# A gated linear attention with an FFN: the rotated q and k of the later groups are turned by transposing DMAs and no longer by TensorE

## The chip, the cores and the metric

The kernel runs on one core of a Trainium2 chip. The metric is the device time of one execution in microseconds (us), lower is better. The times compared are of runs classed as fast (the executions of one kernel lie within 1.5% of each other). Engines: PE is TensorE (matmuls), PEld its weight load, DVE is VectorE, ACT is ScalarE, POOL is GpSimd, SP is SyncE, which in this kernel only issues DMAs.

## The reference

It is a linear attention with a complex decay per channel, of which only the real part of the state is read, followed by a gated FFN on the same tokens. Sizes: 4 batches, 8 heads, 768 steps, head size 48; so 3072 tokens of 384 columns; FFN width 1536. All in float32, with a wide tolerance that lets the kernel work in bf16.

```python
# attention, per batch and head
mag = sqrt(a_re**2 + a_im**2)
scale = minimum(mag, 0.999) / (mag + 1e-6)
a = (a_re + 1j * a_im) * scale
for t in range(S):
    state = a[t][:, None] * state + outer(k[t], v[t])
    y[t] = q[t] @ state.real
# FFN on x = y, heads side by side
g = x @ w_gate
ffn = (gelu(g) * (x @ w_val)) @ w_out
out = x + sigmoid(x @ w_res) * ffn
```

## The kernel before

The kernel cuts the tokens into 12 groups of 256 (two chunks of 128; three groups are one batch) and works in units of one or two groups: [0], [1, 2], [3, 4], [5, 6], [7, 8], [9, 10], [11]. The decay is taken into q and k: with the running sum of log-magnitudes and of phases, each q becomes a pair (cosine and sine part) of 96 columns a head, "rotated" q and k. Within a chunk the attention is then a plain masked product: scores = K Q^T, masked, times v.

Two kinds of stretch alternate. In a **gate/value stretch** (`phase_y(u)`) PE does the gate and value matmuls of unit u, and woven between them are the products and the attention of unit u + 1. In the stretch between two of them (`phase_x`) ACT works out logarithms, exponentials, arctangents and sines for the next unit, small DMAs move decays across partitions, and PE does the output matmuls.

The scores need Q and K with the 96 rotated columns on the partitions, but DVE makes them with tokens on the partitions. So both are turned. Before, TensorE does it, four heads at a time: eight transposes into one PSUM tile, an ACT copy of the q half and a DVE copy of the k half back to SBUF.

```python
pQ = ctx.enter_context(tc.tile_pool(name="pQ", bufs=2))
stt = ctx.enter_context(tc.tile_pool(name="stt", bufs=2))
xp = ctx.enter_context(tc.tile_pool(name="xp", bufs=10))
ldv = ctx.enter_context(tc.tile_pool(name="ldv", bufs=6))
# ... (other pools cut)

def products(g):                        # x0 and x1 (qE = q*E, kE = k/E) cut
    def mk(nm, src):
        def x():
            t = pQ.tile([128, C * H, 2, D], BF, tag=nm, name=nm)
            sb = T[src, g].rearrange("p (x u d) -> p x u d", u=1, d=D).to_broadcast([128, C * H, 2, D])
            nc.vector.tensor_tensor(out=t, in0=T["CS", g], in1=sb, op=OP.mult)
            T[nm, g] = t
        return x
    return [x0, mk("Q", "qE"), x1, mk("K", "kE")]

# attention(g, c): four heads of one chunk
def a():
    tp = psT.tile([128, 1024], BF, tag="tp", name="tp")
    for j in range(4):
        x = c * H + hg * 4 + j
        nc.tensor.transpose(out=tp[0:DD, j * 128:j * 128 + 128], in_=Q(x), identity=ident)
    for j in range(4):
        x = c * H + hg * 4 + j
        nc.tensor.transpose(out=tp[0:DD, 512 + j * 128:640 + j * 128], in_=K(x), identity=ident)
    qk = sqp.tile([128, 1024], BF, tag="qk", name="qk")
    nc.scalar.copy(out=qk[0:DD, 0:512], in_=tp[0:DD, 0:512])
    nc.vector.tensor_copy(out=qk[0:DD, 512:1024], in_=tp[0:DD, 512:1024])
    st["qk", hg] = qk
    at = psA.tile([128, 4, 128], FP, tag="at", name="at")
    for j in range(4):
        nc.tensor.matmul(out=at[:, j], lhsT=qk[0:DD, 512 + j * 128:640 + j * 128],
                         rhs=qk[0:DD, j * 128:j * 128 + 128], start=True, stop=True)
    atm = sqp.tile([128, 4, 128], BF, tag="atm", name="atm")
    nc.vector.tensor_tensor(out=atm, in0=at, in1=mask4, op=OP.mult)

# phase_y(u): gv = gate/value matmuls of unit u, pr = products of unit u + 1;
# the pairs say over which part of the stretch the steps of a list are spread
weave((0.0, 1.0, gv), (0.0, 0.4, pr), (0.3, 0.95, att_steps(u + 1, 0)))
```

The attention steps are emitted at high priority, and a scheduler orders each engine's instructions, so the places in the weave are not the final order.

## Time and profile before

| | before |
|---|---|
| time, median of 4 runs | 323.69 us (322.99 to 324.14) |
| PE / DVE / ACT busy | 84% / 73% / 65% of a span of 322.4 us |
| TensorE transposes of Q and K (`tp`) | 384, in sets of eight |
| gate/value stretches with two turned groups | 26.0, 26.4 and 26.3 us, PE busy 99.6 to 100% |

These are lines of the profile page of the kernel before: busy time of each engine; the granted TensorE clock in 40 slices of the span (tenths, 9 is full speed); the DMA queue that SP feeds (packets, MB, share of 16 engines' time); and four groups of instructions (line, engine, operation, output<-input, shapes, count | busy us, mean ns | idle before).

```profile
PE 272.1 (84%) x2200; PEld 170.5 (53%) x2200; DVE 234.8 (73%) x431; ACT 209.8 (65%) x353; POOL 80.5 (25%) x115
...
PEclk9995676959999999999999999999999999999998
...
q1 hardware_dynamic: 103296, 23.60, 36.8%
...
L351 ACT COPY qk<-tp 96x512 bf16<-96x512 bf16 x48 | 27.9, 580 | 17.1 <-PE tp L349 7.9
...
L346 PE MATMUL tp<-ident,Q 128*96 128x128 bf16 x192 | 20.1, 231 | 6.9 <-DVE Q L321 6.2
...
L349 PE MATMUL tp<-ident,K 128*96 128x128 bf16 x192 | 22.3, 235 | 0.0
...
L352 DVE COPY qk<-tp 96x512 bf16<-96x512 bf16 x48 | 19.8, 413 | 2.3 <-ACT qk L351 1.7
```

The page says what exists, but not what limits. That is read from the windows view: two gate/value stretches of the kernel before (147 and 192 us), each with the stretch after it. The columns are the window, its length, busy time of each engine with its number of instructions, granted clock, DMA share and GB/s.

```profile
core 0: us, PE busy (x) PEld busy (x) DVE busy (x) ACT busy (x) POOL busy (x), PEclk, DMA share, GB/s
147.02:173.00 25.98, 25.87 (x265) 16.04 (x263) 22.85 (x41) 16.91 (x30) 8.60 (x9) 1.00 0.61 77
173.00:192.59 19.59, 17.00 (x85) 9.59 (x84) 14.27 (x29) 17.14 (x28) 10.64 (x15) 1.00 0.54 84
192.59:218.95 26.36, 26.36 (x271) 15.99 (x269) 23.37 (x43) 16.70 (x30) 1.88 (x3) 1.00 0.23 37
218.95:236.33 17.38, 15.42 (x80) 8.69 (x79) 12.56 (x25) 13.51 (x21) 6.89 (x10) 1.00 0.29 56
```

In a gate/value stretch PE is busy for the whole of it at full clock. What a set of transposes really costs in PE's stream is read from PE's timeline (start us, us, engine, line, operation, output<-input, count), because the 231 ns of one transpose overlap with the next:

```profile
198.77 0.39 PE L346 MATMUL tp<-ident,Q 128*96 128x128 bf16 x4
199.00 0.39 PE L349 MATMUL tp<-ident,K 128*96 128x128 bf16 x4
199.22 0.39 PE L356 MATMUL at<-qk 96*128 96x128 bf16 x4
199.44 0.38 PE L443 MATMUL vp<-xT,wv 128*128 128x512 bf16 x1
```

Starts are 0.22 us apart: four transposes take 0.22 us of the stream, so a set of eight takes 0.445 us.

### The profile page before, as it was taken

The numbers are of one execution on the slowest core, as the hardware profiler recorded it, in microseconds if no ns is written. First come the engines' busy times: TensorE is split into PE (matmuls) and PEld (weight loads), VectorE is DVE, ScalarE is ACT, GpSimd is POOL, SyncE is SP. The second block draws the span as 40 slices with busy tenths as digits, with TensorE's granted clock in tenths as the row PEclk, the third lists the DMA queues.
The fourth block names the chain that finished last, engine by engine and source line by source line (L and its number), as shares of the span: only waits on it lengthen the run. The fifth ranks groups of instructions, "written<-read, shape, count | busy, mean of one in ns | idle before, by whom it ended". The sixth has DMA issues, their size and how long they took to land.

```text
span 322.4 us, 5853 instructions
## 1 busy us (share of the span) xinstructions
PE 272.1 (84%) x2200; PEld 170.5 (53%) x2200; DVE 234.8 (73%) x431; ACT 209.8 (65%) x353; POOL 80.5 (25%) x115
## 2 busy tenths in 40 slices
PE   0337927789887999789997999998999999899994
PEld 0116624677543666445664556554656655555682
DVE  2446769968499995599982999974899837864352
ACT  4549684646998557977568976569665683656150
POOL 1206522022040370259020572000630003200220
PEclk9995676959999999999999999999999999999998
DMA  8999999989999995396850595000360003600441
GB/s 159 218 183 181 182 169 165 185 174 180 187 179 186 223 160 33 76 197 113 122 36 2 107 121 95 2 0 3 75 122 3 2 0 76 122 2 0 107 91 50
DMA packets 137755, 34.55 MB, mean 107 GB/s; under 512 B 126848, under 2 KB 137728, under 8 KB 137728
## 3 DMA queue, kind: packets, MB, share of 16 engines
q1 hardware_dynamic: 103296, 23.60, 36.8%
q0 software_dynamic: 34432, 10.59, 31.2%
q8 instruction: 17, 0.28, 0.3%
q14 instruction: 10, 0.08, 0.1%
HBM read 31.31 MB, written 9.07 MB: 125 GB/s over the span
## 4 chain that ended last, share of the span: by engine, by line
PE 56%; SPq 12%; ACT 11%; DMA 9%; DVE 6%; issue 3%; POOL 1%; ACTq 0%; DVEq 0%; POOLq 0%
PE vp L443 14%; PE gp L439 13%; SPq L136 6%; SPq L144 6%; PE op L463 6%; DMA k<-in_k_dram 4%; PE rp L455 3%; PE tp L349 3%; PE tp L346 3%; PE at L356 3%; ACT L477 3%; DMA m<-dm 3%; ACT s L124 3%; PE cst L236 2%; PE y L394 2%
## 5 line engine op out<-in xcount | busy, mean ns | idle before, releaser
L124 ACT ACTIVATE h<-gp 128x512 bf16<-128x512 f32 (+1 forms) x84 | 44.5, 536 | 38.4 <-PE gp L439 37.9
L439 PE MATMUL gp<-xT,wg 128*128 128x512 bf16 (+1 forms) x252 | 65.4, 353 | 3.4 <-ACT h L124 2.0
L443 PE MATMUL vp<-xT,wv 128*128 128x512 bf16 (+1 forms) x252 | 66.6, 353 | 0.0
L446 DVE SCALAR_TENSOR_TENSOR h<-h,vp 128x512 bf16<-128x512 bf16 (+1 forms) x84 | 49.8, 603 | 16.4 <-PE vp L443 12.0
L463 PE MATMUL op<-wo,h 128*128 128x384 bf16 x288 | 50.2, 326 | 8.1 <-ACT Ei L124 5.9
L463 PEld LDWEIGHTS <-h 128*128 128x128 bf16 x288 | 27.8, 98 | 28.7 <-issue 11.3
L351 ACT COPY qk<-tp 96x512 bf16<-96x512 bf16 x48 | 27.9, 580 | 17.1 <-PE tp L349 7.9
L359 DVE TENSOR_TENSOR atm<-at,mask 128x512 bf16<-128x512 f32 x48 | 32.9, 686 | 8.2 <-PE at L356 7.8
L472 POOL DMA_DIRECT2D out_dram<-x x22 | 20.4, 947 | 54.4 <-DMA out_dram<-ot 43.1
L439 PEld LDWEIGHTS <-wg 128*128 128x128 bf16 x252 | 23.7, 99 | 17.9 <-issue 4.2
L443 PEld LDWEIGHTS <-wv 128*128 128x128 bf16 x252 | 23.8, 99 | 13.3
L189 DVE TENSOR_TENSOR ai<-s,ai 128x768 f32<-128x768 f32 x12 | 11.1, 955 | 23.6 <-ACT s L124 23.6
L477 ACT ACT_TABLE_LOAD x21 | 26.9, 1283 | 1.1 <-PEq L615 0.7
L346 PE MATMUL tp<-ident,Q 128*96 128x128 bf16 x192 | 20.1, 231 | 6.9 <-DVE Q L321 6.2
L346 PEld LDWEIGHTS <-Q 128*96 128x96 bf16 x192 | 17.4, 130 | 15.3 <-DVE Q L321 10.0
L124 ACT ACTIVATE CS<-fg,hpi 128x768 bf16<-128x768 f32 x12 | 11.2, 935 | 20.8 <-DVE fg L246 20.7
L150 POOL DMA_DIRECT2D v<-in_v_dram x24 | 21.9, 932 | 4.2 <-DMA v<-in_v_dram 1.3
L349 PE MATMUL tp<-ident,K 128*96 128x128 bf16 x192 | 22.3, 235 | 0.0
L236 PE MATMUL cst<-ai,lt0b 128*128 128x384 f32 x24 | 11.8, 577 | 11.7 <-ACT ai L124 11.0
L352 DVE COPY qk<-tp 96x512 bf16<-96x512 bf16 x48 | 19.8, 413 | 2.3 <-ACT qk L351 1.7
L212 PE MATMUL csl<-ar,lt0a 128*128 128x384 f32 x24 | 11.4, 562 | 10.8 <-DMA ar<-in_a_re_dram 10.8
L466 DVE SCALAR_TENSOR_TENSOR ot<-sg,op 128x384 f32<-128x384 f32 x24 | 13.1, 547 | 10.1 <-PE op L463 10.1
(85 smaller groups left out, 522.0 us busy)
## 6 DMA issues: line engine op xcount, KB each, us to landing
ar<-in_a_re_dram SPq DMA_DIRECT2D x24, 192.0 KB, 4.7
ai<-in_a_im_dram SPq DMA_DIRECT2D x24, 192.0 KB, 4.1
q<-in_q_dram SPq DMA_DIRECT2D x24, 192.0 KB, 3.8
k<-in_k_dram SPq DMA_DIRECT2D x24, 192.0 KB, 3.7
out_dram<-ot SPq DMA_DIRECT2D x24, 192.0 KB, 2.5
out_dram<-x POOLq DMA_DIRECT2D x22, 192.0 KB, 3.7
v<-in_v_dram POOLq DMA_DIRECT2D x24, 96.0 KB, 5.0
wg<-in_moe_w_gate_dram POOLq DMA_DIRECT2D x4, 288.0 KB, 11.4
```

Source lines behind the costliest of these rows:

```text
L124: tab(nc.scalar.activation(**kw))
L150: nc.gpsimd.dma_start(out=t[:, c], in_=rows(v, g, c))
L346: nc.tensor.transpose(out=tp[0:DD, j * 128:j * 128 + 128], in_=Q(x), identity=ident)
L349: nc.tensor.transpose(out=tp[0:DD, 512 + j * 128:640 + j * 128], in_=K(x), identity=ident)
L351: nc.scalar.copy(out=qk[0:DD, 0:512], in_=tp[0:DD, 0:512])
L359: nc.vector.tensor_tensor(out=atm, in0=at, in1=mask4, op=OP.mult)
L439: nc.tensor.matmul(out=gp, lhsT=wg[:, fi, ffi * 128:(ffi + 1) * 128], rhs=xT[:, fi, :], start=(fi == 0), stop=(fi == KD - 1))
L443: nc.tensor.matmul(out=vp, lhsT=wv[:, fi, ffi * 128:(ffi + 1) * 128], rhs=xT[:, fi, :], start=(fi == 0), stop=(fi == KD - 1))
L446: nc.vector.scalar_tensor_tensor(out=h2[:, ffi, :], in0=h2[:, ffi, :], scalar=0.5, in1=vp, op0=OP.mult, op1=OP.mult)
L463: nc.tensor.matmul(out=ps, lhsT=h2[:, ffi, jj * 128:(jj + 1) * 128], rhs=wo[:, ffi, :], start=(ffi == 0), stop=(ffi == KF - 1))
L472: nc.gpsimd.dma_start(out=out[t0:t0 + 128, :], in_=T["x", token(u, jj)], accum_op=OP.add)
L477: tab(nc.scalar.preload_act_table_set(nm))
```

## The change

The intent is to take the turning of q and k off TensorE, ACT and DVE. DVE now writes every group's Q and K into tiles padded from 96 to 128 columns a head. From the sixth group on (g >= 5; seven of twelve groups) one transposing DMA each, issued by SP, turns a whole group's Q or K (128 x 2048 bf16, 512 KB) into `QT` or `KT`. The scores read these. The first five groups are still turned by TensorE; in their part of the span, to about 104 us, the slices show the DMA engines 80% busy and more with loads.

The padded and the turned tiles need SBUF, so the change also makes room: the mask is kept once and broadcast, the phase sums carried from group to group run in a single tile `R`, one temporary is written into its consumer's tile, `G` is a single buffer, and the pools of v and x shrink.

```diff
-    xp = ctx.enter_context(tc.tile_pool(name="xp", bufs=10))
+    xp = ctx.enter_context(tc.tile_pool(name="xp", bufs=8))
-    ldv = ctx.enter_context(tc.tile_pool(name="ldv", bufs=6))
+    ldv = ctx.enter_context(tc.tile_pool(name="ldv", bufs=5))
+    trp = ctx.enter_context(tc.tile_pool(name="trp", bufs=1))
+    pads = {}                           # two per Q and K; pad columns set to zero once
     ...
     def x():                            # products
-        t = pQ.tile([128, C * H, 2, D], BF, tag=nm, name=nm)
+        t = pads[nm, g % 2][:, :, 0:DD].rearrange("p x (u d) -> p x u d", u=2)
         nc.vector.tensor_tensor(out=t, in0=T["CS", g], in1=sb, op=OP.mult)
         T[nm, g] = t
+        if g >= TURN:                   # TURN = 5
+            tt = trp.tile([128, C * H, 128], BF, tag=nm + "T", name=nm + "T")
+            nc.sync.dma_start_transpose(out=tt, in_=pads[nm, g % 2])
+            T[nm + "T", g] = tt
     ...
+    def turned():                       # scores of four heads, in place of a()
+        x0 = c * H + hg * 4
+        st["qk", hg] = T["QT", g][0:DD, x0:x0 + 4]
+        for j in range(4):
+            nc.tensor.matmul(out=at[:, j], lhsT=T["KT", g][0:DD, x0 + j], rhs=T["QT", g][0:DD, x0 + j], ...)
+        nc.vector.tensor_tensor(out=atm, in0=at, in1=mask4, op=OP.mult)
     ...
     if s > 0:                           # carry(g): phase sum ahead of group g
-        P = stt.tile([128, DM], FP, tag="P", name="P")
-        nc.vector.tensor_tensor(out=P, in0=T["th", g - 1][:, DM:W], in1=T["th", g][:, 0:DM], op=OP.add)
-        if s > 1:
-            nc.vector.tensor_tensor(out=P, in0=P, in1=T["P", g - 1], op=OP.add)
+        P = T["R"]                      # one tile, updated again after the group's sums (carry_on)
+        nc.vector.tensor_tensor(out=P, in0=P, in1=T["th", g][:, 0:DM], op=OP.add)
     ...
-    cst = [call(carry, g) for g in g1] + [call(cs_t, g, c) for g in g1 for c in range(C)]
+    cst = [f for g in g1 for f in [call(carry, g)] + [call(cs_t, g, c) for c in range(C)]]
```

More of the change, by code (lines that the diff above doesn't have):

```diff
@@ L59 @@
     I2PI = 1.0 / (2.0 * math.pi)
+    TURN = 5
     LNMAX = 0.5 * math.log(0.998001)
@@ L82 @@
     nc.vector.memset(ones1, 1.0)
-    mask4 = singles.tile([128, 4, 128], BF, name="mask4")
-    for jm in range(4):
-        nc.vector.tensor_copy(out=mask4[:, jm, :], in_=lmat[1])
+    mask1 = singles.tile([128, 1, 128], BF, name="mask1")
+    nc.vector.tensor_copy(out=mask1[:, 0, :], in_=lmat[1])
+    mask4 = mask1.to_broadcast([128, 4, 128])
     wg = singles.tile([128, KD, FF], BF, name="wg")
@@ L90 @@
     wr = singles.tile([128, KD, DM], BF, name="wr")
+    pads = {}
+    for nm in ("Q", "K"):
+        for i in range(2):
+            pads[nm, i] = singles.tile([128, C * H, 128], BF, name="pad%s%d" % (nm, i))
+            nc.gpsimd.memset(pads[nm, i][:, :, DD:128], 0.0)
     lda = ctx.enter_context(tc.tile_pool(name="lda", bufs=6))
     ldq = ctx.enter_context(tc.tile_pool(name="ldq", bufs=4))
-    ldv = ctx.enter_context(tc.tile_pool(name="ldv", bufs=6))
+    ldv = ctx.enter_context(tc.tile_pool(name="ldv", bufs=5))
     pS = ctx.enter_context(tc.tile_pool(name="pS", bufs=2))
@@ L101 @@
     stt = ctx.enter_context(tc.tile_pool(name="stt", bufs=2))
+    st1 = ctx.enter_context(tc.tile_pool(name="st1", bufs=1))
+    trp = ctx.enter_context(tc.tile_pool(name="trp", bufs=1))
     mp = ctx.enter_context(tc.tile_pool(name="mp", bufs=3))
-    xp = ctx.enter_context(tc.tile_pool(name="xp", bufs=10))
+    xp = ctx.enter_context(tc.tile_pool(name="xp", bufs=8))
     xtp = ctx.enter_context(tc.tile_pool(name="xtp", bufs=2))
@@ L222, in carry, with carry_on @@
         if s > 0:
-            P = stt.tile([128, DM], FP, tag="P", name="P")
-            nc.vector.tensor_tensor(out=P, in0=T["th", g - 1][:, DM:W], in1=T["th", g][:, 0:DM], op=OP.add)
-            if s > 1:
-                nc.vector.tensor_tensor(out=P, in0=P, in1=T["P", g - 1], op=OP.add)
+            P = T["R"]
+            nc.vector.tensor_tensor(out=P, in0=P, in1=T["th", g][:, 0:DM], op=OP.add)
             T["P", g] = P
+    def carry_on(g):
+        s = g % NS
+        if s == 0:
+            T["R"] = st1.tile([128, DM], FP, tag="R", name="R")
+            nc.vector.tensor_copy(out=T["R"], in_=T["th", g][:, DM:W])
+        elif s < NS - 1:
+            nc.vector.tensor_tensor(out=T["R"], in0=T["R"], in1=T["th", g][:, DM:W], op=OP.add)
     def cs_t(g, c):
@@ L241, in cs_t @@
         hs = slice(c * H, (c + 1) * H)
-        r = pS.tile([128, H, D], FP, tag="r", name="r")
+        r = fg[:, hs, 0, :]
         nc.vector.tensor_scalar(out=r, in0=cs3, scalar1=MAGIC, scalar2=MAGIC, op0=OP.add, op1=OP.subtract)
@@ L245, in cs_t @@
         if c == C - 1:
+            carry_on(g)
             nc.vector.tensor_scalar(out=fg[:, :, 0, :].bitcast(mybir.dt.int32), in0=fg[:, :, 1, :].bitcast(mybir.dt.int32),
@@ L341, in grp @@
         def grp(hg):
+            def turned():
+                x0 = c * H + hg * 4
+                st["qk", hg] = T["QT", g][0:DD, x0:x0 + 4]
+                at = psA.tile([128, 4, 128], FP, tag="at", name="at")
+                for j in range(4):
+                    nc.tensor.matmul(out=at[:, j], lhsT=T["KT", g][0:DD, x0 + j], rhs=T["QT", g][0:DD, x0 + j],
+                                     start=True, stop=True)
+                atm = sqp.tile([128, 4, 128], BF, tag="atm", name="atm")
+                nc.vector.tensor_tensor(out=atm, in0=at, in1=mask4, op=OP.mult)
+                st["atm", hg] = atm
             def a():
+                if g >= TURN:
+                    turned()
+                    return
                 tp = psT.tile([128, 1024], BF, tag="tp", name="tp")
@@ L352, in a @@
                 nc.vector.tensor_copy(out=qk[0:DD, 512:1024], in_=tp[0:DD, 512:1024])
-                st["qk", hg] = qk
+                st["qk", hg] = qk[0:DD, 0:512].rearrange("p (j t) -> p j t", j=4)
                 at = psA.tile([128, 4, 128], FP, tag="at", name="at")
@@ L367, in enter @@
             Mb = T["M", g][0:DD].rearrange("p (h u) -> p h u", u=1).to_broadcast([DD, H, D])
-            G = stt.tile([128, H, D], FP, tag="G", name="G")
+            G = T["G"] if s > 1 else st1.tile([128, H, D], FP, tag="G", name="G")
             if s == 1:
@@ L395, in yy @@
                 if not first:
-                    nc.tensor.matmul(out=ys, lhsT=st["qk", hg][0:DD, j * 128:j * 128 + 128],
+                    nc.tensor.matmul(out=ys, lhsT=st["qk", hg][:, j],
                                      rhs=T["Gbf"][0:DD, h], start=False, stop=True)
```

## The prediction

> **What bounds the kernel now.** To about 104 us the loads weigh most (slices: DMA 80% busy and more). Then two kinds of stretch alternate. In the gate/value stretches (104-127, 147-173, 192-219, 236-263, 276-297 us) the windows view has PE busy 99.5 to 100%, at clock 1.00, with DVE near 23 us and ACT near 17 us of about 26.5; the timeline shows matmuls back to back: PE's stream is the limit there. Between them (127-147, 173-192, 219-236, 263-276 us) the chain of waits runs through ACT's Ln/Exp/table loads, the small decay transfers (3 us each) and the output matmuls. The `tp` tile's busy tenths put all TensorE transposes of groups 5 to 11 in the PE-bound stretches.
>
> **What the change removes.** From group 5 on: 7 groups x 4 half-chunks = 28 sets. Per set: 8 PE transposes (219 ns duration each, but the chain shows 0.22 us for four back to back, so 0.445 us a set), one ACT copy (580 ns), one DVE copy (413 ns). In sum 12.5 us of PE, 16.2 us of ACT, 11.6 us of DVE. The PE part lies wholly on the critical path: 3.6 us in each of the stretches with two turned groups (three of them), 1.8 us in the last. ACT and DVE don't limit there.
>
> **What it adds.** 14 transposing DMAs on SP's queue, 512 KB each (128 x 2048 bf16; a quarter is padding). The trace has none. The Trainium skill, "DMA: Bandwidth & Descriptors", Latency and other measured facts, gives a transposing DMA 261 GB/s where it isn't contiguous, and a fixed cost of about 2 us: my estimate from it: 2 us of transfer each, 4 us to landing, 6 to 7 us from the Q product until both are there. Plain 192 KB stores here land in 2.5 us. The DMA engines are idle enough (17 to 23% busy after 200 us). The running sum R serialises two groups' phase sums; under 1 us a stretch. Fewer x and v buffers should not bind.
>
> **Is the latency covered?** The new order of PE puts 6 to 8 us of gate/value work between a unit's first Q product and its first masked-score matmul, and 5 to 6 us between the last reader of the single QT buffer and the next group's scores. At 2 us of transfer there is nearly no stall. Each further us costs about 2 us at each of 7 hand-overs, as Q and K go one after the other: at about 3.3 us of transfer (160 GB/s) the whole gain is gone.
>
> **Prediction.** 323.9 - 12.5 + about 3 (stalls on the second group's turn, the serialised sums) = 314.5 us; 8 in 10: 307 to 326 us. Faster by over 2%: 0.63; within 2%: 0.24; slower by over 2%: 0.13.
>
> **What would show it.** The three full gate/value stretches shrink from 26.5 to about 23.5 us with PE still near 100%; PE busy falls by about 12, ACT by 16, DVE by 11 us; the stretches between them keep their 13 to 19 us; transposing DMAs land in 4 to 5 us; PE's waits on them come to under 4 us in total.
>
> **What would make it wrong.** A transposing DMA much slower than plain (PE waits several us on KT/QT at each hand-over; the gate/value stretches grow); transposes holding SP's queue, so that stores and loads come late; output adds releasing the 8 x buffers late; the R chain lengthening the stretches between.

## The result, and the profile after

| | before | after |
|---|---|---|
| time, median of 4 runs | 323.69 us (322.99 to 324.14) | 343.19 us (341.75 to 343.37) |
| ratio to before, 95% interval | | 1.0593 (1.0568 to 1.0619) |
| PE / DVE / ACT busy | 272.1 / 234.8 / 209.8 us | 266.5 / 226.3 / 194.8 us |
| mean granted clock of the profiled run | 0.949 | 0.912 |

A ratio is the mean time of one kernel's fast runs over that of the other's of the same rounds, so it is not quite the ratio of the medians in the tables.

The kernel became 19.5 us slower. The work did leave the engines: ACT fell by 15.0 us and DVE by 8.5. PE fell by 5.6 us only, which already looks odd against the 12.5 expected (and 19 of PE's 1976 matmuls have no record in this trace, so it fell by somewhat less). The page of the kernel after, same lines as above, with the new score matmuls in place of the old turning:

```profile
PE 266.5 (78%) x1957; PEld 161.0 (47%) x1976; DVE 226.3 (66%) x404; ACT 194.8 (57%) x325; POOL 81.4 (24%) x119
...
PEclk9955757879999999997898997998999999999998
...
q1 hardware_dynamic: 132416, 30.94, 47.3%
...
L368 PE MATMUL at<-QT,KT 96*128 96x128 bf16 x112 | 13.2, 235 | 21.5 <-DMA KT<-padK 15.2
```

PE was idle for 21.5 us just before the 112 score matmuls that read the turned tiles. The waits view of the kernel after (engine, line, what it waited for: us in total, times, longest us) splits this into seven waits, one per turned group. DVE's 30.6 us belong to the same waits, one step later: its mask needs the scores.

```profile
DVE atm L371 <- PE at L368: 30.6, 14, 5.9
...
PE at L368 <- DMA KT<-padK: 15.2, 5, 5.8
...
PE at L368 <- DMA QT<-padQ: 6.3, 2, 4.9
```

The second thing is in the clock row: before, the digits after the first quarter are all 9; after, there are 7s and 8s in the middle. The windows view of the kernel after shows both. The first four rows are the same stretches as those shown of before; the last five are short windows at three of the waits, the last two of them after these stretches.

```profile
core 0: us, PE busy (x) PEld busy (x) DVE busy (x) ACT busy (x) POOL busy (x), PEclk, DMA share, GB/s
148.49:184.82 36.33, 25.46 (x189) 13.77 (x190) 19.15 (x32) 12.07 (x21) 8.12 (x9) 0.86 0.84 112
184.82:206.87 22.05, 19.58 (x99) 10.66 (x98) 17.63 (x34) 17.29 (x28) 10.58 (x15) 1.00 0.61 100
206.87:236.59 29.72, 24.91 (x198) 13.32 (x202) 19.65 (x33) 12.55 (x23) 2.07 (x3) 0.89 0.50 84
236.59:252.31 15.72, 14.20 (x73) 8.12 (x72) 11.88 (x22) 13.40 (x22) 6.46 (x10) 1.00 0.19 40
...
160.30:164.40 4.10, 4.10 (x23) 2.17 (x24) 2.15 (x3) 0.60 (x1) 0.00 (x0) 0.50 0.53 106
173.70:178.60 4.90, 0.00 (x0) 0.00 (x1) 0.00 (x0) 0.41 (x1) 0.00 (x0) 0.99 1.30 120
178.60:181.20 2.60, 2.57 (x19) 1.78 (x20) 1.38 (x2) 0.48 (x1) 0.00 (x0) 0.50 0.00 0
...
258.40:262.00 3.60, 0.10 (x1) 0.00 (x1) 0.43 (x1) 0.00 (x0) 0.85 (x1) 1.00 1.02 175
262.00:273.40 11.40, 11.29 (x97) 6.26 (x99) 9.77 (x16) 5.47 (x10) 0.00 (x0) 1.00 0.51 96
```

The gate/value stretch that was 26.0 us is 36.3, the one of 26.4 is 29.7. PE's busy time in the first is hardly less than before (25.5 against 25.9 us), although 76 matmul records fewer fall in it, because after the two long waits PE worked at half clock, for 4.1 and 2.6 us. (The share of busy DMA counts a packet by its duration, so a window can exceed 1.)

Each gate/value stretch taken with the one after it, as the order of work shifts between the two: 45.6 us became 58.4 (+12.8), 43.7 became 45.4 (+1.7), 38.4 became 40.0 (+1.6), the rest of the span 47.7 became 48.9 (+1.2); and all before it took 1.5 us more. So two thirds of the loss lie in one pair, and in no pair was anything won.

Why PE waits is read from SP's timeline of the kernel after, in that first stretch (start us, us that SP was held by the issue, what was issued):

```profile
148.01 2.21 SPq L342 DMA_TRANSPOSE QT<-padQ  x1
150.32 1.23 SPq L505 DMA_DIRECT2D out_dram<-ot  x1
151.65 2.27 SPq L342 DMA_TRANSPOSE KT<-padK  x1
154.01 3.33 SPq L153 DMA_DIRECT2D q<-in_q_dram  x2
163.12 0.99 SPq L153 DMA_DIRECT2D k<-in_k_dram  x2
168.20 1.77 SPq L342 DMA_TRANSPOSE KT<-padK  x1
170.06 2.58 SPq L342 DMA_TRANSPOSE QT<-padQ  x1
```

and from PE's timeline, at the two waits (in brackets: idle before, and what ended it):

```profile
160.26 0.61 PE L368 MATMUL at<-QT,KT 96*128 96x128 bf16 x4 [5.80 <-DMA KT<-padK]
...
178.63 0.59 PE L368 MATMUL at<-QT,KT 96*128 96x128 bf16 x4 [4.93 <-DMA QT<-padQ]
```

First wait: DVE had finished the Q product at 147.98 and the K product at 149.39. SP was held 2.2 us by issuing the turn of Q, then issued an output store, and only at 151.65 the turn of K, which landed 8.57 us later (the chain of waits has this piece). From the Q product until both were there it took 12.2 us; PE had work for 6.5 us of it.

Second wait: the Q product of the next group was ready at 155.05, but there is only one `QT` tile, and the last matmuls that read it started at 169.07. So this group's turn of Q was issued at 170.06 and landed at 178.5. PE had other work until 173.7. The first wait had also delayed this group's K product, as DVE's timeline shows (its mask of the first scores stood ahead of that product, and DVE waited with PE):

```profile
154.10 0.95 DVE L338 TENSOR_TENSOR padQ<-CS,qE 128x1536 bf16<-128x1536 bf16 x1
160.90 0.69 DVE L371 TENSOR_TENSOR atm<-at,mask 128x512 bf16<-128x512 f32 x1 [5.86 <-PE at L368]
...
167.18 0.95 DVE L338 TENSOR_TENSOR padK<-CS,kE 128x1536 bf16<-128x1536 bf16 x1
```

So the turn of K was issued only at 168.20 and held SP until 169.97, just before the turn of Q.

The transposing DMAs of the kernel after in the DMA view (output<-input, queue, operation, count, median us from issue to landing):

```profile
QT<-padQ SPq DMA_TRANSPOSE x7, 5.7
KT<-padK SPq DMA_TRANSPOSE x7, 5.5
```

The shortest took 4.3 us, the longest 8.6.

### The profile page after: what moved, and what is told of

Read it like the earlier page. It is cut to its first block, busy times and chain, and to the rows that moved or that the text cites. A ratio compares the mean times of both kernels' runs of the same rounds, so it can differ in the third digit from the quotient of the medians.

```text
span 341.2 us, 5355 instructions
## 1 busy us (share of the span) xinstructions
PE 266.5 (78%) x1957; PEld 161.0 (47%) x1976; DVE 226.3 (66%) x404; ACT 194.8 (57%) x325; POOL 81.4 (24%) x119
## 3 DMA queue, kind: packets, MB, share of 16 engines
q1 hardware_dynamic: 132416, 30.94, 47.3%
## 4 chain that ended last, share of the span: by engine, by line
PE 39%; DMA 16%; DVE 13%; issue 12%; SPq 9%; ACT 8%; POOL 0%; DVEq 0%; ACTq 0%; POOLq 0%
PE vp L478 9%; PE gp L474 8%; DMA KT<-padK 7%; PE op L498 6%; SPq L145 5%; DMA k<-in_k_dram 4%; SPq L153 3%; PE rp L490 3%; ACT s L133 3%; DMA QT<-padQ 2%; PE cst L252 2%; PE at L368 2%; DVE fg L260 2%; ACT L512 2%; DVE fg L259 2%
## 5 line engine op out<-in xcount | busy, mean ns | idle before, releaser
L474 PE MATMUL gp<-xT,wg 128*128 128x512 bf16 (+1 forms) x236 | 66.2, 365 | 2.7 <-DVE xT L465 1.6
L478 PE MATMUL vp<-xT,wv 128*128 128x512 bf16 (+1 forms) x249 | 65.9, 363 | 0.2
L371 DVE TENSOR_TENSOR atm<-at,mask 128x512 bf16<-128x512 f32 x28 | 19.2, 687 | 30.6 <-PE at L368 30.6
L478 PEld LDWEIGHTS <-wv 128*128 128x128 bf16 x252 | 24.8, 102 | 20.5 <-issue 3.2
L368 PE MATMUL at<-QT,KT 96*128 96x128 bf16 x112 | 13.2, 235 | 21.5 <-DMA KT<-padK 15.2
L368 PEld LDWEIGHTS <-KT 96*128 96x128 bf16 x112 | 9.3, 106 | 27.7 <-DMA KT<-padK 17.7
L429 PE MATMUL y<-v,atm 128*128 128x48 bf16 x192 | 19.9, 192 | 1.6 <-DVE atm L394 1.6
L252 PE MATMUL cst<-ai,lt0b 128*128 128x384 f32 x24 | 11.0, 540 | 12.9 <-ACT ai L133 10.9
L429 PEld LDWEIGHTS <-atm 128*128 128x128 bf16 x192 | 14.6, 101 | 11.6 <-DVE atm L371 5.3
L501 DVE SCALAR_TENSOR_TENSOR ot<-sg,op 128x384 f32<-128x384 f32 x24 | 13.1, 548 | 9.4 <-PE op L498 6.5
L180 POOL COPY landed<-k 1x1 f32<-1x1 f32 x10 | 4.8, 484 | 57.9 <-DMA k<-in_k_dram 57.9
```

What stands on the lines that cost most here:

```text
L252: nc.tensor.matmul(out=cs, lhsT=tmat[c], rhs=th[:, sl], start=True, stop=(s == 0))
L368: nc.tensor.matmul(out=at[:, j], lhsT=T["KT", g][0:DD, x0 + j], rhs=T["QT", g][0:DD, x0 + j], start=True, stop=True)
L429: nc.tensor.matmul(out=ys, lhsT=st["atm", hg][:, j], rhs=V(h), start=True, stop=first)
L474: nc.tensor.matmul(out=gp, lhsT=wg[:, fi, ffi * 128:(ffi + 1) * 128], rhs=xT[:, fi, :], start=(fi == 0), stop=(fi == KD - 1))
L478: nc.tensor.matmul(out=vp, lhsT=wv[:, fi, ffi * 128:(ffi + 1) * 128], rhs=xT[:, fi, :], start=(fi == 0), stop=(fi == KD - 1))
```

## The experiments

Three explanations stood against each other. Theory A: PE waits for the turned tiles, so the loss is the latency of the turn, and the gain from the removed PE work is real but hidden. The rivals: the rest of the change (running sum, fewer buffers, order of the phase sums) costs the time; or the DMAs' own load, on SP's queue and on the DMA engines, does it by delaying other transfers, without PE having to wait for the turned tiles.

Times below are medians; where a kernel is run beside the one before, that one took 323.6 to 323.9 us. Edits are against the changed kernel.

### never: all of the change except the turning

```diff
-    TURN = 5
+    TURN = 99
```

> The changed kernel with no group turned by DMA: all groups go through TensorE again, but the padded tiles, the running sum R, the broadcast mask and the smaller pools stay. Theory A (the loss is PE waiting for transposing DMAs that land late): back at the time of before, 322 to 326 us. Rival B (the loss comes from the other parts of the change): 335 us or more.

Measured: 325.53 us, ratio 1.0071 (1.0031 to 1.0112), correct. So the rest of the change costs about 2 us, not 20.

### unused: the DMAs run, the scores use TensorE's transposes

The transposing DMAs are issued as in the change, but no one reads what they write.

```diff
-                if g >= TURN:
+                if g >= 99:
                     turned()
```

> The 14 transposing DMAs are issued as in the changed kernel, but nobody reads what they write; the scores go through TensorE as before. Theory A: 323 to 328 us, as nothing waits for them. Rival C (the transposes hold the SP queue and the DMA engines, so that loads and stores come late): 333 us or more.

Measured: 325.91 us, ratio 1.0052 (1.0036 to 1.0069), correct. Next to `never` the fourteen DMAs add nothing that can be told apart. As long as PE neither waits for them nor runs faster, their traffic is free.

### nowait: the scores read a weight tile, the DMAs run unread

Its output is wrong, which doesn't matter for the time. PE's and DVE's work is that of the change, but nobody waits for `QT` and `KT`.

```diff
-    st["qk", hg] = T["QT", g][0:DD, x0:x0 + 4]
+    st["qk", hg] = wg[0:DD, 0, 0:512].rearrange("p (j t) -> p j t", j=4)
-    nc.tensor.matmul(out=at[:, j], lhsT=T["KT", g][0:DD, x0 + j], rhs=T["QT", g][0:DD, x0 + j], ...)
+    nc.tensor.matmul(out=at[:, j], lhsT=wg[0:DD, 1, j * 128:j * 128 + 128], rhs=wg[0:DD, 0, j * 128:j * 128 + 128], ...)
```

> Wrong result on purpose: the turned groups take weights that landed long before as their turned q and k, and the 14 transposing DMAs still run, unread. So the TensorE transposes and their copies are gone and nothing waits. Theory A: the full saving of 12.5 us shows, 310 to 315 us. Rival C: 320 us or more. If PE's work in the gate/value stretches was not what set their length, 318 us or more as well.

Measured: 320.8 us, ratio 0.9911 (0.9883 to 0.9938). 22 us of the loss are gone, but theory A had expected 310 to 315 us: a miss of at least 6 us. Its waits view names what is new:

```profile
ACT x L434 <- DMA out_dram<-x: 8.7, 3, 5.0
```

ACT could not write an attention output into an x tile, because the tile was still being added to the output by a DMA. That DMA landed after 8.4 us instead of the usual 4, in a stretch with a DMA share of 0.99; PE then waited 4.0 us for ACT, and after this wait it ran 6.3 us at a clock of 0.54 (2.9 us lost). So the DMAs' load does cost something once PE's stream is faster, which `unused` could not show.

### micro: the transposing DMA by itself

A program with nothing but DMAs, each waiting for the one before; then four transposes in a row and four plain copies in a row. Its output is wrong, which doesn't matter for the time.

```python
for nm, blocks in (("sixteen", 16), ("eight", 8), ("four", 4), ("single", 1), ("plain", 0)):
    for i in range(4):
        t = one.tile([128, blocks or 16, 128], BF, tag="t", padded_shape=[128, 16, 128], name=nm)
        if blocks:
            nc.sync.dma_start_transpose(out=t, in_=src[:, 0:blocks])
        else:
            nc.sync.dma_start(out=t, in_=src)
# then four of each kind into tiles of their own: rowturna to d, rowcopya to d
```

> Wrong result on purpose: only DMAs, one waiting for the other: four transposes each of 16, 8, 4 and 1 blocks of 128 columns (512, 256, 128, 32 KB), four plain copies of 512 KB from SBUF to SBUF, then four transposes of 512 KB in a row without waits and four plain copies. If the transpose alone is slow (theory A): 512 KB takes 4 us or more to landing alone, four in a row take 2.8 to 3.2 us each (from the 3.05 us of 16 engines that the changed kernel's trace shows per transpose), and the issue takes over 1.5 us on SP. If it was only crowded by other transfers: about 2 us each in a row, 3.5 us alone, issue under 1 us.

Measured, in the DMA view:

```profile
plain<-src SPq DMA_DIRECT2D x4, 512.0 KB, 2.9
...
sixteen<-src SPq DMA_TRANSPOSE x4, 4.3
eight<-src SPq DMA_TRANSPOSE x4, 3.1
...
single<-src SPq DMA_TRANSPOSE x4, 2.2
```

"sixteen" is the DMA of the change. Alone it lands in 4.3 us, close to the 4 us of the prediction. Two sizes give its slope: 256 KB more cost 1.2 us. But SP is held 1.8 us by issuing it (0.47 us for the plain copy), and four in a row land about 2.4 us apart (7.3 us from the first landing to the last), so each further one costs about 2.4 us (about 215 GB/s), not 2. The plain copies in a row land 1.3 us apart (406 GB/s in the 2.4 us from 77.5). Alone and in its issue the DMA is thus as slow as theory A expected here; in a row it lies between the two expectations (2.8 to 3.2 us, and about 2).

### free: no transposing DMA and the full buffers

As `nowait`, with the DMAs left out and the pools of x and v at 10 and 6 buffers. Its output is wrong, which doesn't matter for the time.

> Wrong result on purpose: as the run without waits, but with no transposing DMA at all and with the former 10 x and 6 v buffers. It asks what the removal is worth when nothing takes its place. If PE's stream is the limit of the gate/value stretches: the time of the run with no group turned (325.5) less 12.5, so 311 to 315 us, and 3.6 us less in each of the three full gate/value stretches. If something else sets their length: above 318 us. The difference to the run without waits (320.8) is what 8 x buffers and the transposes' traffic cost.

Measured: 312.72 us, ratio 0.9654 (0.9604 to 0.9703). This is about the most that the idea can give (`best`, below, comes 0.8 us lower, about the spread of the runs): a hit. Two of its gate/value stretches took 22.2 and 22.7 us in place of 26.4 and 26.3. The 12.5 us of PE do lie on the critical path.

### free8: the same with the change's smaller pools

As `free`, with 8 and 5 buffers (to split the miss of `nowait`).

> Wrong result on purpose: as the run in which nothing takes the place of the TensorE transposes, but with the changed kernel's 8 x and 5 v buffers. It parts the 8.1 us between that run (312.7) and the run without waits (320.8). If the fewer buffers cost it: 318 to 321 us, with ACT waiting several us for an output add to free an x buffer. If the transposes' traffic made those adds late: 312 to 314 us, without that wait.

Measured: 312.67 us, ratio 0.9659 (0.9626 to 0.9692). Fewer buffers alone cost nothing. `nowait` differs from `free8` only by the fourteen DMAs, so those 8.1 us are the DMAs' load, which makes the output adds late; with eight x buffers that stops ACT. The wait of 4.0 us and the 2.9 us of lost clock after it are most of the 8.1. Whether ten x buffers would have absorbed it was not tried.

### turn7: two groups fewer are turned by DMA

```diff
-    TURN = 5
+    TURN = 7
```

> The changed kernel, but DMA turns only from the eighth group on (TURN 7), so the stretch with the loads still under way keeps TensorE's transposes. Theory A with crowding: that stretch gives back its 10 us excess, 331 to 335 us; the others keep their waits. If the stall were the same at every hand-over whatever else the DMA carries: 4 of 14 transposes fewer give back only 4/14 of the 19.5 us, about 337 us.

Measured: 335.85 us, ratio 1.0370 (1.0302 to 1.0439), correct; 14.1 us of waits for `QT` and `KT` are left. The first stretch, with its crowded DMA engines, is now free of turns, but the loss falls by 7.3 us only, between the two expectations: the next two stretches grew to 30.8 and 31.0 us. So the crowding of the first stretch explains a part, not the whole.

### hold6: the scores are put off

The DMAs stay as in the change. The attention steps of turned units start at 0.6 of the stretch, and the scheduler is bound not to take the first score matmul of a turned group ahead of the gate/value matmul emitted before it.

```diff
-        weave((0.0, 1.0, gv), (0.0, 0.4, pr), (0.3, 0.95, att_steps(u + 1, 0)))
+        at0 = 0.6 if gs(u + 1) and gs(u + 1)[0] >= TURN else 0.3
+        weave((0.0, 1.0, gv), (0.0, 0.4, pr), (at0, 1.0 if at0 > 0.3 else 0.95, att_steps(u + 1, 0)))
     ...
+                    if j == 0 and hg == 0 and c == 0 and "gv" in T:     # i: the score matmul
+                        tc.add_manual_dep(i.ins, T["gv"].ins.name, order, reason="after gate/value work")
     ...
-            nc.tensor.matmul(out=vp, ...)
+            T["gv"] = nc.tensor.matmul(out=vp, ...)
```

> The changed kernel with one thing moved: a unit's first scores may start only after the gate/value step that the program has reached by then, which puts 4.5 us more of PE work in front of the first wait of each unit; the hand-over to the second group stays as it was. Theory A: the four first waits (5.8, 1.7, 3.5 and 2 us, 13 us in all) shrink to about 1 us, and the half clock after them goes too, so 325 to 330 us. If the loss did not come from waiting there: 340 us or more.

Measured: 321.79 us, ratio 0.9941 (0.9879 to 1.0002), correct; better than expected. Nothing but the order changed, and 21 us came back. Its waits view:

```profile
PE at L368 <- DMA QT<-padQ: 7.0, 3, 3.9
...
PE at L368 <- DMA KT<-padK: 1.4, 1, 1.4
```

8.4 us of waits instead of 21.5. What is left is mostly the other hand-over: the second group's turn, which waits for the single `QT` (7.0 us). The new order also freed DVE: the second group's K product, which in the changed kernel came only at 167.2 us, behind a mask that waited for PE, is made at 157.2. How much of the 21 us is due to this was not parted.

### split: the DMAs are cut by chunk

Each turn is cut in two (one per chunk of 128 tokens, 256 KB), each into a half tile of its own with two buffers, so that the same SBUF holds the halves and the first half of the next group can be turned while the second of this one is read. Issued in the order Q and K of the first chunk, Q and K of the second.

```diff
-    trp = ctx.enter_context(tc.tile_pool(name="trp", bufs=1))
+    trp = ctx.enter_context(tc.tile_pool(name="trp", bufs=2))
-                    tt = trp.tile([128, C * H, 128], BF, tag=nm + "T", name=nm + "T")
-                    nc.sync.dma_start_transpose(out=tt, in_=pads[nm, g % 2])
-                    T[nm + "T", g] = tt
+                    pend_t.append((nm, g))
+                    if nm == "K":
+                        for c in range(C):
+                            for n2, g2 in pend_t:
+                                tt = trp.tile([128, H, 128], BF, tag=n2 + "T", name=n2 + "T")
+                                nc.sync.dma_start_transpose(out=tt, in_=pads[n2, g2 % 2][:, c * H:(c + 1) * H])
+                                T[n2 + "T", g2, c] = tt
+                        pend_t.clear()
```

> The cut in two halves with two buffers, without the hold. The order of PE now puts the first scores of a unit 1.7 us earlier than in the changed kernel, but only the first halves of Q and K need to have landed, and the second group's first half may be turned earlier. Theory A: less waiting than in the changed kernel, but not none, 326 to 336 us. If hold and split did the same thing twice, split alone would already give the 316 us of both.

Measured: 333.20 us, ratio 1.0297 (1.0256 to 1.0338), correct. Half of the waits (11.6 us in seven, all on `KT`) and 10 us of the time came back: about one wait of 1.7 us remains at each group. Cutting alone does not cover the latency. The edit makes the pieces smaller and gives them two buffers at once; which of the two helped was not parted.

### splithold6: both

The edits of `split` and `hold6` together.

> The same hold, and each transposing DMA cut in two by 128-token chunk, with two buffers of half the size, so that the next group's first half may be turned while the second half of this one is still read. Theory A: both waits mostly vanish, 314 to 320 us, faster than before. If SP's issue of twice as many transposes (1.2 us each for 256 KB alone) outweighs this: 324 us or more.

Measured: 316.16 us, ratio 0.9768 (0.9716 to 0.9820), correct. 1.8 us of PE waits on turned tiles are left. The interval reaches over the 2% line, so "faster by over 2%" is not certain here. The two remedies add up to less than their sum (27.0 us against 21.4 and 10.0), as each covers some of the same wait.

### neverP: never, with the running sum's reader decoupled

`never` left about 2 us unexplained. Here the phase sum that the matmuls read gets a tile of its own again (in the slots of `qk`, so that no SBUF is added), and the old order of the phase sums is back.

```diff
+        P = sqp.tile([128, DM], FP, tag="qk", padded_shape=[128, 512], name="P")
+        nc.vector.tensor_tensor(out=P, in0=T["R"], in1=T["th", g][:, 0:DM], op=OP.add)
+        if s < NS - 1:
+            nc.vector.tensor_tensor(out=T["R"], in0=P, in1=T["th", g][:, DM:W], op=OP.add)
     ...
-        cst = [f for g in g1 for f in [call(carry, g)] + [call(cs_t, g, c) for c in range(C)]]
+        cst = [call(carry, g) for g in g1] + [call(cs_t, g, c) for g in g1 for c in range(C)]
```

> No group turned by DMA, and the running phase sum put into its own tile for each group, so that TensorE's reading of one group's sum no longer holds back the next addition; the order of the phase matmuls as before. If the 1.6 us that the run with no group turned lost against before came from the serialised sum: 323 to 324.5 us, and the stretch at 173 us takes 19.6 us again, not 21.7. If it came from the padding, the mask or the smaller pools: 325 us or more, unchanged.

Measured: 325.16 us, ratio 1.0046 (1.0020 to 1.0072), correct. A miss of the expected 323 to 324.5, and the stretch at 173 us takes 21.1 us (171.5 to 192.7), not 19.6, though more of PE's work falls in it now. The interval overlaps that of `never`, so a cost of the serialised sum is not shown; between the two runs lie 0.4 us, and their intervals leave room for some 2 us. Where the remaining 1.6 us of the rest of the change come from stays open.

### best: split, a milder hold, and the separate sum

The edits of `split` and `neverP` (with TURN = 5) and the hold of `hold6` with the start at 0.4 of the stretch in place of 0.6.

> Split, hold and the sum in its own tile together. If the parts add up: 1 to 2 us below the 316.2 us of split and hold, so 313.5 to 315.5 us, near the 312.7 us of the run in which nothing takes the place of the transposes. If the serialised sum does not matter here: 316 us again.

Measured: 311.93 us (311.25 to 312.76, five runs) against 323.56, ratio 0.9641 (0.9621 to 0.9661), correct. It beats both kernels and lies below both expectations. No PE wait on `QT` or `KT` is left in its waits view, and its windows, for the same stretches as above, show it:

```profile
core 0: us, PE busy (x) PEld busy (x) DVE busy (x) ACT busy (x) POOL busy (x), PEclk, DMA share, GB/s
147.06:168.18 21.12, 20.75 (x171) 11.08 (x169) 18.29 (x29) 11.73 (x20) 8.68 (x9) 1.00 1.29 189
...
188.79:209.78 20.99, 20.33 (x172) 11.05 (x170) 19.14 (x33) 11.73 (x21) 1.85 (x3) 1.00 0.83 137
```

PE is nearly full again and at full clock, in stretches of 21 us instead of 26. With the stretches between them the span fell by 12.6 us, which is the 12.5 us of PE that the change removes. Nor does ACT wait for an output add here, although the DMAs move the same 30.94 MB on SP's queue with eight x buffers: the 8.1 us of `nowait` are no fixed price of the load. As three edits act at once here, and the hold is a milder one than in `splithold6`, the run shows what they reach together, not the share of each.

## Why the prediction was wrong

It said 314.5 us (307 to 326); the result was 343.19 us. Point by point:

- **What bounds the kernel: right.** PE's stream limits the gate/value stretches (26.0 to 26.4 us, PE 99.6 to 100% busy), and `free` and `best` gave back just what was removed from it.
- **What the change removes: right.** 12.5 us of PE were estimated; `free` is 10.9 us faster than before, with what the rest of the change costs (about 2 us) still in it, and the span of `best` is 12.6 us shorter. ACT fell by 15.0 us (16.2 estimated) and DVE by 8.5 (11.6 estimated): DVE's copies did fall by 11.6 us (19.8 to 8.2), but the phase sums in `R` take 1.4 us more, and the rest was not traced. PE's busy time on the page fell by 5.6 us only, as half-clock work takes twice as long; in `best`, without the half clock, it is 259.0 us, 13.1 less than before.
- **The rest of the change: right within its size.** About 2 us (`never` 325.5), against "under 1 us a stretch" for the sum; fewer buffers are free by themselves (`free8`).
- **The DMA alone: right.** 4.3 us to landing, 4 estimated.
- **"Is the latency covered?": this is the step that failed.** The prediction put the waits at "under 4 us in total" and booked "about 3" us for stalls and sums. PE waited 21.5 us, at each of the seven hand-overs. `hold6` changed only the order and got 21 us back, and `nowait` took away the waiting and got 22 back, so this cause is shown.

Three terms of that step were too small:

1. *The turn itself.* 2 us of transfer were estimated per DMA; alone in a row it is 2.4 us (`micro`). In the kernel the queue's share of the DMA engines grew from 36.8% of 322.4 us to 47.3% of 341.2 us, that is 42.7 us of all sixteen engines, 3.05 us for each of the fourteen. This counts packets by their duration, and counted so the four in a row of `micro` take 2.8 us each (0.96 of 11.8 us), so the kernel's other traffic added little. By the prediction's own rule (2 us at each of seven hand-overs for each further us of transfer) 2.4 us would have cost 6 us more and 3.05 us 15 more. The result was 29 us above 314.5, so this term alone is not enough.
2. *The way from the product to both tiles.* 6 to 7 us were estimated, as if issue cost nothing and the path were free. SP was held 1.6 to 4.2 us by one issue, an output store came between Q and K, and in the first stretch loads and output adds shared the engines, so landing took 8.4 to 8.6 us. It came to 12.2 us in the first stretch and 9.0 us in the second. PE had work for 6.5 us in the first, so the cover was read rightly (6 to 8 us) and what it had to cover was not.
3. *The single tile.* The prediction saw 5 to 6 us between the last reader of `QT` and the next scores, and took that to be enough for 2 us of transfer. But the whole latency must fit, not the transfer: from 169.1 to 178.5 us, with 4.6 us of other work for PE. `split`, which lets the halves overlap, halved the waits.

Not foreseen at all was the **clock**. After three of the waits PE ran at half or two-thirds clock: 4.1 us and 2.6 us at 0.50, 5.0 us at 0.66. The missing share times the length is 2.1 + 1.3 + 1.7 us. Another 4.7 us at 0.64 (from 208.8 us, 1.7 us lost) follow short idle times at the start of a stretch and come just before a wait on `KT`, so these are not shown to come from such waits. Together about 7 us. In `best` the clock is 1.00 in all the gate/value stretches after 147 us. The sum: 323.7 - 12.5 + 21.5 + about 7 + about 2 = 342, against 343.2 measured. This adds up parts that were read from traces; no run parted the clock from the waits.

The prediction's list of what would make it wrong held the cause, "PE waits several us on KT/QT at each hand-over"; it gave too little weight to it. "Output adds releasing the 8 x buffers late" was seen too, but only when the waits were gone (`nowait`, 8.1 us); it does not explain the result.

How this reads beside the Trainium skill:

- "DMA: Bandwidth & Descriptors", section Latency and other measured facts, gives 261 GB/s for a transposing DMA that isn't contiguous, on which the estimate rested. Here it was about 215 GB/s in a row alone (`micro`).
- "TensorE: Matmul & The Clock Gate", section Why this matters for your kernels, says to leave PE no idle gaps above some 3 us, as an idle window throws the clock back to half. The trace agrees for the waits of 5.8 and 4.9 us (0.50 after them). A gap of 3.6 us (258.4 to 262.0) lost nothing, which fits with its statement, in What's actually happening, that the window runs freely. Reading this page for what a stall would bring, and not only for matmul speed, would have put a price on the waits.

## What to carry to other kernels

Moving work from a full engine to a DMA trades throughput for latency, so ask at every hand-over how long the consumer has other work, and count the whole way against it: the issue on its queue, what is queued before it, the landing in a crowded stretch, and the wait for a free destination tile. Here the gain was real but hidden by 21.5 us of waits; cutting the transfer into pieces with two buffers and putting the consumers later in the stream (and, in the last run, a phase sum in its own tile) turned a 5.9% loss into a 3.6% gain with the same DMA traffic. Count a PE wait of several us at more than its length, because the clock may be halved after it.

## What the Trainium skill lacked or had wrong

- "Advanced Engine Details and Errata", X-Bar Transpose (TRN2), says that transposing DMAs are as fast as regular ones, at 350 to 400 GB/s. Here, SBUF to SBUF with 256-byte packets, four in a row cost about 2.4 us each for 512 KB (about 215 GB/s), plain copies of the same size 1.3 us each (406 GB/s); alone, 4.3 against 2.9 us to landing.
- No page gives in so many words how long a transposing DMA holds its issuing engine on this chip; "DMA: Bandwidth & Descriptors" counts the sequencer's cycles only for another chip and for "previous generations" that it does not name. Alone it was 1.8 us for 512 KB, 1.2 us for 256 KB and 1.1 us for 32 KB, against 0.47 us for a plain copy; in the busy kernel 1.6 to 4.2 us. It delays every later DMA of that queue.
- "VectorE: DVE Perf Modes", The three transpose paths, gives 1309 ns for one 128x128 block by DMA and 390 ns by TensorE. A single block took 2.2 us from issue to landing here (the page does not say from where to where it counts); TensorE's transposes of 128x96 streamed at 55 ns each (0.22 us for four), with 219 ns duration of one. For a kernel with many blocks the streamed figure counts.
- "TensorE: Matmul & The Clock Gate", What's actually happening, ties the loss of clock to an idle window of about 3.4 us. In the kernel after, a gap of 1.9 us (226.7 to 228.6) was followed by 5.0 us at 0.66, and 1.4 us of idle time in pieces (206.0 to 208.8) by 4.7 us at 0.64; what else led to these was not tested.
